# ScalarE's copies spread by an account of its work, one more transform with eight residues, and the last inverse rows moved by six products

## The chip, the cores and the metric

The kernel runs on one core of one Trainium2 chip. The metric is device time in microseconds of one launch. The core's engines run side by side, each with an instruction stream of its own: TensorE (PE, with its weight loads as PEld), VectorE (DVE), ScalarE (ACT), GpSimd (POOL) and SyncE (SP). SP, ACT and POOL also issue the DMAs.

## The reference, cut to what matters

The kernel computes the forward and the backward pass of a block with two branches: a long convolution over the sequence (branch A) and a bilinear gated unit (branch B).

```python
xn = layernorm(q)                                   # 2048 x 1024
k_shift = sum over t of k_pad[t:t+S] * shift_k[:, 3-t]
kv = k_shift * v
y  = irfft(rfft(kv, 4096) * rfft(ssm_k, 4096))[:S] + kv * ssm_D
s  = xn * y                                         # branch A
h  = (xn @ w_gate) * (xn @ w_up)                    # 2048 x 3584
g  = silu(h @ w_down)                               # branch B
out = q + s * g
# the outputs: out, and the gradients of all inputs for a given grad_out
```

## The kernel before

**Stages.** The program is a sequence of dense matmul stages on TensorE. The convolution's Fourier transforms and products, most of which are VectorE's work, run beside them. The stage around the change is the first one: the gate and up projections (`gu_unit`, 14 slabs of 256 columns of F, 16 blocks of 128 rows each), with the forward convolution (`conv_forward`) beside it. After it comes the down projection (`bm_mm`, `late_mm`), under which the last slice of the convolution ends.

**A product.** `gu_unit` takes one to four row blocks of one slab. For each it makes a *product*: eight matmuls of 128x512 into one of two PSUM buffers `psg` (L671), which ScalarE copies into `gut` (L673). TensorE can start a product only when the copy of the product two before is done. Four products on, VectorE multiplies gate by up into `hN` (recorded at L212 as `hN<-gut`), `Hd` and `GUd` are stored, and for a pair of units `turn_pair` (L694 to L706) turns `hN` on TensorE through the one PSUM tile `tr`; two ScalarE copies bring it to `hT`, which SP stores in `HTd`. The turn is put off by five products (`defer`, `flush(5)`).

**The convolution.** It goes over eight slices of 128 columns (`ds` 0 to 7). A slice needs the transform of kv (kind 0) and that of the filter row h (kind 1). Each transform has two halves: TensorE multiplies by Fourier tables into `psF` tiles (`cmm`, L234), two ScalarE copies bring a half to one of two `SP` buffers (L256 or L295), and VectorE sums them (`W<-SP`) and forms the spectrum in `KX` or `HX`. With four residues (`fwd4_half`) a transform is 32 matmuls of 128x256 and little VectorE work; with eight (`fwd8_half`) it is 16 and more VectorE work. `EIGHT` lists the transforms that use eight. After the product of both spectra (`product`) comes the inverse on VectorE (`inv_dft` or `inv8`), and then `tail`: inverse rows on TensorE into `psI` (L455) and ScalarE's copies to `yf` (L825).

**The filter row.** Before its transform, h is ordered by four ScalarE copies `hx<-U` (`h_order`, L785), turned on TensorE through `tr`, and copied back by two `hx<-tr` (`h_turn`, L809). For slice 0, `h_turn` transposes straight from the row (L800, copies L802). Both are called from the stages of `product`: `h_order` in its first four, `h_turn` in the fifth.

**What sets the order.** The convolution is a generator that yields its estimated VectorE time. `tick`, called once per product, pumps it by a fraction of the total `F_TOTAL`. That order is the program order. A scheduler may move instructions on their engines by its own estimate, except those given to `tc.keep_in_program_order`: once `PIN[0]` is set, VectorE's of the convolution, and the first matmul of each group of a transform. ScalarE's copies are not pinned.

**The end of the convolution.** When the projections end, VectorE still works on slice 7. TensorE goes on with products of the down projection: `late_mm(n)` is the n-th, two matmuls of 128x512. The inverse rows of slice 7 are issued by `step()` behind products 68 and 75 (`at`), each followed by copies to `yf` and `y_first` on ScalarE. The gates, VectorE's next stage, need these rows.

Of the kernel before, what the change touches and what calls it, by code (L numbers as in the profile page):

```python
# [10 lines left out]
ACT = mybir.ActivationFunctionType  # L11
# [8 lines left out]
def build_kernel(  # L20
# [11 lines left out]
    nc = tc.nc  # L32
# [27 lines left out]
    def ld(out, in_):  # L60
        return nc.sync.dma_start(out=out, in_=in_)
# [9 lines left out]
    def sta(out, in_):  # L71
        return nc.scalar.dma_start(out=out, in_=in_)
# [113 lines left out]
    def turn_tables(psp):  # L186

        for j in range(2):
            ps = psp.tile([P, 8, 2, P], BF16, name="psT", tag="psF")
            for r in range(8):  # L190
                for k in range(2):
                    nc.tensor.transpose(ps[:, r, k, :], T4[j][:, r, k, :], ident[:])
            nc.scalar.copy(out=TI[:, j], in_=ps[:])
            yield


# [32 lines left out]
    def cmm(ps, T, x, rs, first=None, held=False):  # L229

        xr = x.rearrange("p (c r) d -> p r c d", c=2)
        for k in range(2):
# [5 lines left out]
            if first is not None and k == 0:  # L238
                nc.tensor.matmul(ps[:, 0, 0:P], T[:, 0, 0, :], first, start=False, stop=True)

    pe_us = [0.0]

    def net(w):
# [4 lines left out]
    def fwd4_half(x, i, wp, psp, first=None):  # L248

        pe_us[0] += 1.75  # L250
        SP = wp.tile([P, 2, 2, 512], F32, name="SP", bufs=2)
        for par in range(2):
            ps = psp.tile([P, 2, 2, 256], F32, name="psF")
            cmm(ps[:, 0], T4[par], x, (i, i + 4), first if i == 0 else None, True)
            cmm(ps[:, 1], T4[par], x, (i + 2, i + 6))
            nc.scalar.copy(out=SP[:, :, par], in_=ps[:].rearrange("p s k x -> p s (k x)"))  # L256
        return SP

    def fwd4_buf(wp):
# [27 lines left out]
    def fwd8_half(x, i, SP, psp, first=None, held=False):  # L287

        pe_us[0] += 0.87
        for j in range(2):  # L290
            r = 2 * i + j
            ps = psp.tile([P, 2, 2, 256], F32, name="psF")
            cmm(ps[:, 0], T4[0], x, (r,), first if r == 0 else None, held)
            cmm(ps[:, 1], T4[0], x, (r + 4,))
            nc.scalar.copy(out=SP[:, :, j], in_=ps[:].rearrange("p s k x -> p s (k x)"))  # L295

    def fwd8(SPs, X, W, C, ahead, late=False):

# [269 lines left out]
    def halves(x):  # L568
        return x.rearrange("p b (h u) -> p h b u", h=2)
# [64 lines left out]
    later = []  # L634
    gu_mm = [None]

    def tr_tile():
        return ps_tr.tile([P, 2, 8, P], BF16, name="tr")

    def defer(fn):  # L640
# [14 lines left out]
    def gu_unit(sl, b0, n, w, tick):  # L655
# [11 lines left out]
        for i in range(n):  # L667
            q, qi = divmod(b0 + i, 4)
            ps = ps_gu.tile([P, 512], F32, name="psg")
            for dc in range(DC):  # L670
                gu_mm[0] = nc.tensor.matmul(ps[:], XNT[q][:, dc, qi * P:(qi + 1) * P],  # L671
                                            w[:, dc].rearrange("p a f -> p (a f)"), start=(dc == 0), stop=(dc == DC - 1))
            nc.scalar.copy(out=gut[:, :, i], in_=ps[:].rearrange("p (a f) -> p a f", a=2))  # L673
            flush(5)
            if i == 0:
                turn_late()
            hn[0]()
            hn[0] = nop
            tick()
        sta(GUd[sl, b0 // 8][:, :, b0 % 8:b0 % 8 + n], gut[:, :, 0:n])  # L680

        def multiply():
# [24 lines left out]

        def store(hT):
            half, rest = divmod(b0, 8)
# [30 lines left out]
    def conv_forward():  # L740
# [12 lines left out]
        def load_h(ds):  # L753
            hrow = U[5][:, 0:2048].rearrange("p (c u r) -> p c u r", c=2, r=8)
            cld(U[5][:, 0:2048], A_ssm_k[ds * P:(ds + 1) * P, :])
            S_["h", ds] = hrow
# [18 lines left out]
            yield 2.3  # L775

        def h_order(ds, part):
            if ds == 8:
                return
            hrow = S_["h", ds]  # L780
            if part == 0:
                S_["hx"] = cf.tile([P, NB, P], BF16, name="hx")
            if ds > 0:
                c, q = divmod(part, 2)
                nc.scalar.activation(S_["hx"][:, 4 * part:4 * part + 4, :], hrow[:, c, :, 4 * q:4 * q + 4].rearrange("p u r -> p r u"),  # L785
                                     ACT.Copy, scale=WSC)
                if part == 3 and ds + 1 < 8:
                    load_h(ds + 1)

        def h_turn(ds):  # L790
            if ds == 8:
                return
            hx = S_["hx"]
            pe_us[0] += 0.67
            if ds == 0:
                hrow = S_["h", 0]
                ps = tr_tile()
                for b in range(NB):
                    with tc.issue_after(tr_ln[0].ins) if b == 0 else nullcontext():
                        nc.tensor.transpose(ps[:, b // 8, b % 8, :], hrow[:, b // 8, :, b % 8], ident[:])  # L800
                    if b % 8 == 7:
                        nc.scalar.activation(hx[:, b - 7:b + 1, :], ps[:, b // 8], ACT.Copy, scale=WSC)  # L802
                load_h(1)
            else:
                ps = tr_tile()[:].rearrange("p h b x -> p h (b x)").rearrange("p h (b u) -> p h b u", u=64)
                for b in range(NB):
                    turn_halves(lambda hh: ps[:, hh, b], hx[:, b, :])
                for c in range(2):
                    nc.scalar.copy(out=halves(hx[:, 8 * c:8 * c + 8, :]), in_=ps[:, :, 8 * c:8 * c + 8])  # L809
            h_out.append(ds)  # L810

        def kvs(ds):
            return S_["kvt", ds // 2][:, :, ds % 2 * P:(ds % 2 + 1) * P]
# [1 line left out]
        def tail(ds):  # L815
            G = S_.pop(("G", ds))
            if ds < 7:
                yf = cs.tile([P, NB, P], BF16, name="yf")[:]
            else:
                yf = krow[:].rearrange("p a b d -> p (a b d)")[:, 0:NB * P].rearrange("p (b d) -> p b d", b=NB)  # L820
            for rq in range(2):
                ps = (ps_tr if cv_gone else ps_cv).tile([P, 4, 256], F32, name="psI", tag="tr" if cv_gone else "psF")
                inv_quad(G, ps, rq, ds in INV8)
                pe_us[0] += 0.9 if ds in INV8 else 1.8
                nc.scalar.copy(out=yf.rearrange("p (c r) d -> p r c d", c=2)[:, 4 * rq:4 * rq + 4], in_=rowps(ps))  # L825
# [50 lines left out]
        yield from shift(0)  # L876
        PIN[0] = True
        yield 3.9
        h_order(0, 0)
        h_turn(0)  # L880
        yield 0.1
        tl = turn_tables(ps_cv)
        sp = [half(0, S_["hx"], i, Dz[:, 0:P]) for i in range(2)]
        for ds in range(8):
# [11 lines left out]
            if ds == 0:  # L896
                yield from transform(0, 1, sp, HX, own_room(KX), lambda i: sph.append(half(0, kvs(0), i)), nop)
            else:
                yield from transform(ds, 0, sp, KX, own_room(HX), lambda i: sph.append(half(ds, S_["hx"], i, D0)), nop)
                S_["kst"] = st(KFd[ds], KX[:])  # L900
            calls = []

# [13 lines left out]
                S_["filters"] = False  # L916
            st(HFd[ds], HX[:])
            for n, w in enumerate(product(KX, HX, KX, cs, False, 0)):
                if n < 4:
                    h_order(ds + 1, n)  # L920
                else:
# [80 lines left out]
    def tick(by=1):  # L1002
        cnt[0] += by
        if cnt[0] == -4:
            pump((SHIFT_W + 4.05) / F_TOTAL)
        if cnt[0] >= -2:
            pump((SHIFT_W + (F_TOTAL - SHIFT_W) * (cnt[0] + 6.5) / (NT + 3.5)) / F_TOTAL)
# [38 lines left out]
                ld(HT0[1][:, 8:12], ht_rows(0, 24, 28))  # L1046
    assert len(h_out) == 8 and not soon
    hn[0]()

    def bm_mm(ps, ht, i, fc):  # L1050
        for dh in range(2):
# [16 lines left out]
    pss = [ps_bm.tile([P, D], F32, name="psbm") for i in range(2)]  # L1068
    with tc.issue_after(bm_first(range(4)).ins):
        flush()  # L1070
    for p_ in (ps_gu, fg, fw):
        p_.release()
    ub = pool("ub", 1, side="right")
# [752 lines left out]
```

## Time and profile before

| what | value |
|---|---|
| median of three runs | 1915.73 us (1915.4 to 1916.0) |
| the profiled execution's time | 1915.55 us |
| its span, first to last instruction | 1913.8 us |
| granted TensorE clock | 1.00 |
| products (`psg`) end | about 505 us |
| VectorE's forward convolution ends | 551.6 us |
| inverse rows of slice 7 | 561.45 and 565.34 us |

A line of the page's fifth part, or of a list of groups, gives the source line, engine, operation, tiles (written <- read), shapes and count, then the busy time and the mean of one, then the engine's idle time before them and what ended it. The costliest ScalarE groups of 100 to 505 us read so:

```profile
L673 ACT CAST gut<-psg 128x512 bf16<-128x512 f32 x131 | 76.8, 591 | 89.9 <-PE psg L671 84.7 <-remote 3.4 <-DVE m L212 1.1
L705 ACT COPY hT<-tr 128x1024 bf16<-128x1024 bf16 x46 | 44.4, 1018 | 0.5 <-PE tr L565 0.5
L256 ACT COPY SP<-psF 128x1024 f32<-128x1024 f32 x44 | 42.5, 1018 | 9.3 <-PE psF L234 6.8 <-DVE W L212 1.8 <-DVE KX L212 0.7
L785 ACT ACTIVATE hx<-U 128x512 bf16<-128x512 bf16 x28 | 31.2, 1167 | 2.5 <-DVE KX L283 2.5
```

A gut copy takes 0.59 us, every other copy about one; a product on TensorE takes 1.73 us (eight matmuls, one each 0.216). In lists in order of time a line gives start and length in us, engine, line, operation, tiles, shapes and count, and in brackets the idle time before it with what ended it.

### The profile page before, as it was taken

What the parts mean: (1) busy time and instruction counts of PE and PEld (TensorE: products, weight loads), DVE (VectorE), ACT (ScalarE), POOL (GpSimd) and SP (SyncE); (2) the same over time, 40 slices, a digit from 0 to 9 for tenths busy, and PEclk for the clock granted to TensorE, in tenths of its full rate; (3) what the DMA queues carried; (4) which work ended last, traced back from release to release, by engine and by line L of the source; (5) the groups of instructions that cost most, each with busy time, mean ns of one, the idle gap of its engine ahead of it and who ended that gap; (6) DMA issues with size and microseconds to landing.
All of it is one profiled execution on the core that took longest, in us unless ns stands there. A gap on an engine that the chain in (4) does not pass through costs nothing.

```text
span 1913.8 us, 28261 instructions
## 1 busy us (share of the span) xinstructions
PE 1890.4 (99%) x11350; PEld 1007.9 (53%) x11491; DVE 1550.6 (81%) x1711; ACT 664.0 (35%) x955; POOL 332.8 (17%) x465
## 2 busy tenths in 40 slices
PE   8999999999999999999999999999999999999999
PEld 5555555545544456666666665664444444444444
DVE  8999999999978556887999999999995205788862
ACT  5765666656433233432222222222222102110121
POOL 5121211201103220001031221111212101111120
PEclk9999999999999999999999999999999999999999
DMA  8777766769769997677887698585887999989862
GB/s 292 273 240 235 259 219 219 234 224 298 249 207 301 326 321 231 209 238 230 273 266 262 223 265 265 182 286 177 226 246 171 228 201 196 186 183 190 187 181 89
DMA packets 425107, 444.35 MB, mean 232 GB/s; under 512 B 268400, under 2 KB 342796, under 8 KB 410512
## 3 DMA queue, kind: packets, MB, share of 16 engines
q1 hardware_dynamic: 367504, 239.03, 46.4%
q0 software_dynamic: 41152, 174.15, 28.9%
q10 hardware_dynamic: 16320, 29.36, 4.1%
q8 instruction: 90, 1.47, 0.3%
q14 instruction: 41, 0.34, 0.1%
HBM read 193.87 MB, written 189.84 MB: 200 GB/s over the span
## 4 chain that ended last, share of the span: by engine, by line
PE 94%; DVE 2%; ACT 2%; issue 1%; DMA 0%; SPq 0%; ACTq 0%
PE psb L1517 20%; PE psx L1662 20%; PE psg L671 17%; PE psb L1500 10%; PE psbm L1052 10%; PE psb L1600 9%; PE psF L234 3%; PE tr L565 1%; PE psI L455 1%; DVE W L212 1%; ACT hx L785 1%; PE psY L1211 1%; PE psY L445 1%; PE psx L1600 1%; DVE bst L578 0%
## 5 line engine op out<-in xcount | busy, mean ns | idle before, releaser
L671 PE MATMUL psg<-wslab,U 128*128 128x512 bf16 x1727 | 398.0, 380 | 12.2 <-ACT gut L673 3.8
L1517 PE MATMUL psb<-U,U 128*128 128x512 bf16 x1792 | 397.1, 379 | 0.0
L1662 PE MATMUL psx<-U,dgut 128*128 128x512 bf16 x1505 | 331.0, 379 | 1.6
L1662 PEld LDWEIGHTS <-dgut 128*128 128x128 bf16 x1792 | 174.9, 98 | 211.8
L1517 PEld LDWEIGHTS <-U 128*128 128x128 bf16 x1792 | 174.9, 98 | 198.3
L671 PEld LDWEIGHTS <-U 128*128 128x128 bf16 x1792 | 172.0, 98 | 203.8 <-issue 9.8
L1500 PE MATMUL psb<-wdt,U 128*128 128x256 bf16 x1792 | 205.6, 273 | 0.0
L1500 PEld LDWEIGHTS <-U 128*128 128x128 bf16 x1792 | 174.8, 98 | 29.6
L212 DVE TENSOR_TENSOR W<-W 128x1024 f32<-128x1024 f32 (+1 forms) x189 | 186.5, 1003 | 4.0
L1600 PE MATMUL psb<-U,U 128*128 128x512 bf16 x797 | 176.1, 380 | 0.9
L1522 ACT CAST wb<-psb 128x512 bf16<-128x512 f32 x112 | 65.7, 587 | 315.3 <-PE psb L1517 307.5
L1267 DVE SCALAR_TENSOR_TENSOR dkp<-dkT,kT 128x1024 bf16<-128x1024 bf16 (+2 forms) x64 | 78.3, 1224 | 94.5 <-DMA dkT<-DKSHd 92.8
L1052 PE MATMUL psbm<-U,ht 128*128 128x512 bf16 x658 | 145.1, 379 | 0.7
L1600 PEld LDWEIGHTS <-U 128*128 128x128 bf16 x896 | 87.2, 98 | 104.5
L1694 ACT ACTIVATE dx_t<-dxn 128x1024 bf16<-128x1024 f32 x15 | 15.9, 1057 | 324.9 <-DVE dxn L212 320.1
L673 ACT CAST gut<-psg 128x512 bf16<-128x512 f32 x156 | 91.4, 592 | 101.9 <-PE psg L671 96.3
L1052 PEld LDWEIGHTS <-ht 128*128 128x128 bf16 x672 | 65.5, 98 | 78.3
L212 DVE TENSOR_TENSOR U<-U,dht 128x2048 bf16<-128x2048 bf16 x56 | 68.3, 1221 | 46.7 <-ACT dht L1502 46.7
L1502 ACT CAST dht<-psb 128x512 bf16<-128x512 f32 x112 | 65.7, 588 | 116.1 <-PE psb L1500 115.0
L66 POOL DMA_DIRECT2D Hd<-hN x54 | 37.1, 687 | 256.8 <-DVE hN L212 254.0
L1641 ACT CAST wbs<-psb 128x512 bf16<-128x512 f32 x51 | 29.9, 587 | 145.4 <-PE psb L1600 134.4
L212 DVE TENSOR_TENSOR W<-SP 128x1024 f32<-128x1024 f32 x64 | 74.3, 1219 | 1.5 <-ACT SP L295 0.8
(265 smaller groups left out, 2361.0 us busy)
## 6 DMA issues: line engine op xcount, KB each, us to landing
U<-GUd SPq DMA_DIRECT2D x28, 1024.0 KB, 9.2
DGd<-U SPq DMA_DIRECT2D x28, 1024.0 KB, 5.9
GUd<-gut ACTq DMA_DIRECT2D x39, 512.0 KB, 6.5
out_dram<-wb SPq DMA_DIRECT2D x112, 128.0 KB, 4.4
U<-Hd SPq DMA_DIRECT2D x14, 1024.0 KB, 5.9
Hd<-hN POOLq DMA_DIRECT2D x54, 256.0 KB, 4.4
HTd<-hT SPq DMA_DIRECT2D x24, 512.0 KB, 4.0
ht<-HTd SPq DMA_DIRECT2D x18, 512.0 KB, 7.8
```

What stands on the lines that cost most here:

```text
L212: pinned(V.tensor_tensor(o, a, b, op))
L234: mm = nc.tensor.matmul(ps[:, k].rearrange("p (c d) -> p c d", c=2), T[:, r, k, :], xr[:, r], start=(n == 0), stop=(n == len(rs) - 1 and ( ...
L671: gu_mm[0] = nc.tensor.matmul(ps[:], XNT[q][:, dc, qi * P:(qi + 1) * P], w[:, dc].rearrange("p a f -> p (a f)"), start=(dc == 0), stop=(dc ...
L673: nc.scalar.copy(out=gut[:, :, i], in_=ps[:].rearrange("p (a f) -> p a f", a=2))
L1052: mm = nc.tensor.matmul(ps[:, dh * 512:(dh + 1) * 512], ht(fc)[:, i * P:(i + 1) * P], WD[fc // 4][:, fc % 4, dh * 512:(dh + 1) * 512], sta ...
L1267: ins = V.scalar_tensor_tensor(prod[:].rearrange("p r d -> p (r d)")[:, lo:H], dkT[:, 0, lo:H], 1.0, kT[:, 0, 13 + m + lo:13 + m + H], op0 ...
L1500: nc.tensor.matmul(ps[:, x * SLW:(x + 1) * SLW], DBMT[2 * hf + g][:, dc, (b % 4) * P:(b % 4 + 1) * P], wdt[:, dc, :], start=(dc == 0), sto ...
L1502: nc.scalar.copy(out=dht[:, 2 * e:2 * e + 2].rearrange("p b f -> p (b f)"), in_=ps[:])
L1517: nc.tensor.matmul(ps[:], XN[b // 4][:, b % 4, dc * P:(dc + 1) * P], dgus[b // 8][:, :, b % 8], start=(b == 0), stop=(b == NB - 1))
L1522: nc.scalar.copy(out=wb[:, dc % 2].rearrange("p a f -> p (a f)"), in_=ps[:])
L1600: nc.tensor.matmul(ps, h[:, f, b, :], DBM[b // 4][:, b % 4, dh * 512:(dh + 1) * 512], start=(b == 0), stop=(b == NB - 1))
L1662: nc.tensor.matmul(ps[:, dh * 512:(dh + 1) * 512], t[n][:, f, i * P:(i + 1) * P], WGU[n][:, f, dh * 512:(dh + 1) * 512], start=(n == 0 and ...
```

## The change

It has three parts.

1. **An account of ScalarE's work.** `act_us` grows with each slow copy (`copied`) and falls by 2.0 per product, to which 0.6 for the gut copy is added (`one_tick`). The copies of h (`h_order`, `h_back`) and of `hT` no longer stand where their data is made: they go into a list `slow`, and after each product `run_slow` issues from it while the account stays under 2.2. The turn of h, too, is issued from that list. Copies of `hT` go to its front. A copy out of the tile `tr` that is still held is issued at once when `tr` is wanted again (`tr_tile`), and one of h when its transform wants it (`hx`). With `PIN[0]` set, these copies and those of gut, SP, TI and yf are kept in program order.
2. **`EIGHT`** gains `(5, 0)`: kv of slice 5 is transformed with eight residues.
3. **`at`** becomes `(74, 81)`: the two groups of inverse rows of slice 7 stand six products of the down projection later.

```diff
+    act_us = [0.0]
+    slow = []
+
+    def copied(us, ins=None):
+        act_us[0] += us
+        if ins is not None and PIN[0]:
+            tc.keep_in_program_order(ins)
+
+    def one_tick():
+        act_us[0] = max(0.0, act_us[0] - 2.0) + 0.6
+
+    def run_slow(all_=False):
+
+        while slow and (all_ or act_us[0] + slow[0][0] < 2.2):
+            us, fn = slow.pop(0)
+            copied(us)
+            fn()
...
-            nc.scalar.copy(out=SP[:, :, par], in_=ps[:].rearrange("p s k x -> p s (k x)"))
+            copied(1.0, nc.scalar.copy(out=SP[:, :, par], in_=ps[:].rearrange("p s k x -> p s (k x)")))
...
+    tr_held = []
+
     def tr_tile():
+        while tr_held:
+            slow.pop(0)[1]()
         return ps_tr.tile([P, 2, 8, P], BF16, name="tr")
...
-            nc.scalar.copy(out=gut[:, :, i], in_=ps[:].rearrange("p (a f) -> p a f", a=2))
+            one_tick()
+            copied(0.0, nc.scalar.copy(out=gut[:, :, i], in_=ps[:].rearrange("p (a f) -> p a f", a=2)))
             flush(5)
...
             tick()
+            run_slow()
...
-            for g in range(2):
-                nc.scalar.copy(out=halves(hT[:, 2 * g:2 * g + 2].rearrange("p q a i s -> p (q a i) s")), in_=ps[:, :, 8 * g:8 * g + 8])
-            ht_st[0] = ld(to.rearrange("q f a s -> f q (a s)"), hT[:].rearrange("f q a i s -> f q (a i s)"))
+
+            def copy(g):
+                copied(0.0, nc.scalar.copy(out=halves(hT[:, 2 * g:2 * g + 2].rearrange("p q a i s -> p (q a i) s")),
+                                           in_=ps[:, :, 8 * g:8 * g + 8]))
+                if g == 1:
+                    tr_held.clear()
+                    ht_st[0] = ld(to.rearrange("q f a s -> f q (a s)"), hT[:].rearrange("f q a i s -> f q (a i s)"))
+            tr_held.append(True)
+            slow.insert(0, (1.0, lambda: copy(1)))
+            slow.insert(0, (1.0, lambda: copy(0)))
...
-    EIGHT = ((0, 0), (0, 1), (6, 0), (7, 0), (7, 1))
+    EIGHT = ((0, 0), (0, 1), (5, 0), (6, 0), (7, 0), (7, 1))
...
+        def h_rows(ds):
+            if ds < 8:
+                pe_us[0] += 0.67
+                for part in range(4):
+                    slow.append((1.15, lambda part=part: h_order(ds, part)))
+                slow.append((0.0, lambda: h_turn(ds)))
+                for c in range(2):
+                    slow.append((1.0, lambda c=c: h_back(ds, c)))
...
+        def hx(ds):
+            while len(h_out) <= ds:
+                slow.pop(0)[1]()
+            return S_["hx"]
...
             for n, w in enumerate(product(KX, HX, KX, cs, False, 0)):
-                if n < 4:
-                    h_order(ds + 1, n)
-                else:
-                    h_turn(ds + 1)
+                if n == 1:
+                    h_rows(ds + 1)
                 yield w
...
-    at = (68, 75)
+    at = (74, 81)
```

The first row of h (slice 0) has a function of its own, `h_first`, with the work of the old `h_turn(0)`. What is left of `slow` is issued at the end of the projections (`run_slow(True)`).

More of the change, by code (lines that the diff above doesn't have):

```diff
@@ L192, in turn_tables @@
                     nc.tensor.transpose(ps[:, r, k, :], T4[j][:, r, k, :], ident[:])
-            nc.scalar.copy(out=TI[:, j], in_=ps[:])
+            copied(1.9, nc.scalar.copy(out=TI[:, j], in_=ps[:]))
             yield
@@ L294, in fwd8_half @@
             cmm(ps[:, 1], T4[0], x, (r + 4,))
-            nc.scalar.copy(out=SP[:, :, j], in_=ps[:].rearrange("p s k x -> p s (k x)"))
+            copied(1.0, nc.scalar.copy(out=SP[:, :, j], in_=ps[:].rearrange("p s k x -> p s (k x)")))
     def fwd8(SPs, X, W, C, ahead, late=False):
@@ L777, in h_order @@
         def h_order(ds, part):
-            if ds == 8:
-                return
-            hrow = S_["h", ds]
             if part == 0:
                 S_["hx"] = cf.tile([P, NB, P], BF16, name="hx")
[L783 to L788, printed above, removed]
@@ L790, in h_turn @@
-        def h_turn(ds):
[L791 to L803, printed above, removed]
-            else:
-                ps = tr_tile()[:].rearrange("p h b x -> p h (b x)").rearrange("p h (b u) -> p h b u", u=64)
-                for b in range(NB):
-                    turn_halves(lambda hh: ps[:, hh, b], hx[:, b, :])
-                for c in range(2):
-                    nc.scalar.copy(out=halves(hx[:, 8 * c:8 * c + 8, :]), in_=ps[:, :, 8 * c:8 * c + 8])
-            h_out.append(ds)
+            c, q = divmod(part, 2)
@@ new lines, in h_order @@
+            copied(0.0, nc.scalar.activation(S_["hx"][:, 4 * part:4 * part + 4, :],
+                                             S_["h", ds][:, c, :, 4 * q:4 * q + 4].rearrange("p u r -> p r u"), ACT.Copy, scale=WSC))
+            if part == 3 and ds + 1 < 8:
+                load_h(ds + 1)
+        def h_turn(ds):
+            ps = tr_tile()[:].rearrange("p h b x -> p h (b x)").rearrange("p h (b u) -> p h b u", u=64)
+            for b in range(NB):
+                turn_halves(lambda hh: ps[:, hh, b], S_["hx"][:, b, :])
+            S_["hps"] = ps
+            tr_held.append(True)
@@ new lines, in h_back @@
+        def h_back(ds, c):
+            copied(0.0, nc.scalar.copy(out=halves(S_["hx"][:, 8 * c:8 * c + 8, :]), in_=S_["hps"][:, :, 8 * c:8 * c + 8]))
+            if c == 1:
+                tr_held.clear()
+                h_out.append(ds)
+        def h_rows(ds):
[4 more added lines that the diff above has]
+                slow.append((0.0, lambda: h_turn(ds)))
+                for c in range(2):
+                    slow.append((1.0, lambda c=c: h_back(ds, c)))
@@ new lines, in h_first @@
+        def h_first():
+            hx = S_["hx"] = cf.tile([P, NB, P], BF16, name="hx")
+            hrow = S_["h", 0]
+            ps = tr_tile()
+            for b in range(NB):
+                with tc.issue_after(tr_ln[0].ins) if b == 0 else nullcontext():
+                    nc.tensor.transpose(ps[:, b // 8, b % 8, :], hrow[:, b // 8, :, b % 8], ident[:])
+                if b % 8 == 7:
+                    nc.scalar.activation(hx[:, b - 7:b + 1, :], ps[:, b // 8], ACT.Copy, scale=WSC)
+            load_h(1)
+            h_out.append(0)
@@ L824, in tail @@
                 pe_us[0] += 0.9 if ds in INV8 else 1.8
-                nc.scalar.copy(out=yf.rearrange("p (c r) d -> p r c d", c=2)[:, 4 * rq:4 * rq + 4], in_=rowps(ps))
+                copied(1.05, nc.scalar.copy(out=yf.rearrange("p (c r) d -> p r c d", c=2)[:, 4 * rq:4 * rq + 4], in_=rowps(ps)))
                 if ds == 7 and rq == 0:
@@ L878, in conv_forward @@
         yield 3.9
-        h_order(0, 0)
-        h_turn(0)
+        h_first()
         yield 0.1
@@ L898, in conv_forward @@
             else:
-                yield from transform(ds, 0, sp, KX, own_room(HX), lambda i: sph.append(half(ds, S_["hx"], i, D0)), nop)
+                yield from transform(ds, 0, sp, KX, own_room(HX), lambda i: sph.append(half(ds, hx(ds), i, D0)), nop)
                 S_["kst"] = st(KFd[ds], KX[:])
@@ L918, in conv_forward @@
             for n, w in enumerate(product(KX, HX, KX, cs, False, 0)):
-                if n < 4:
-                    h_order(ds + 1, n)
-                else:
-                    h_turn(ds + 1)
+                if n == 1:
+                    h_rows(ds + 1)
                 yield w
@@ L1048, in build_kernel @@
     hn[0]()
+    run_slow(True)
     def bm_mm(ps, ht, i, fc):
@@ L1070, in build_kernel @@
         flush()
+        run_slow(True)
     for p_ in (ps_gu, fg, fw):
```

## The prediction

> **What bounds the kernel now.** I read the page's busy line, then busy time by stage, then the waits that ended TensorE's idle time in the stage that the change touches, then stretches in order of time.
>
> ```profile
> PE 1890.4 (99%) x11350; PEld 1007.9 (53%) x11491; DVE 1550.6 (81%) x1711; ACT 664.0 (35%) x955; POOL 332.8 (17%) x465
> ...
> PEclk9999999999999999999999999999999999999999
> ```
> ```profile
> 125.00:555.00 430.00, 424.02 (x3039) 223.64 (x3092) 423.84 (x395) 251.60 (x333) 62.87 (x89) 1.00 0.73 244
> ```
> TensorE sets the time, at full clock. But from 125 to 555 us (columns: PE, PEld, DVE, ACT, POOL) VectorE is as full: 423.84 of 430. ScalarE, 59% busy, can only hurt by its order. The waits (us, times, longest) from 50 to 570 us:
> ```profile
> PE psg L671 <- ACT gut L673: 2.9, 4, 1.5
> PE psg L671 <- ACT U L673: 2.5, 3, 1.4
> ```
> Seven waits, 5.4 us: a product (eight matmuls) finds both psg buffers uncopied. One of them, TensorE first, then ScalarE:
> ```profile
> 109.17 1.89 PE L671 MATMUL psg<-wslab,U 128*128 128x512 bf16 x8 [1.39 <-ACT U L673]
> ```
> ```profile
> 105.75 1.14 ACT L785 ACTIVATE hx<-U 128x512 bf16<-128x512 bf16 x1
> 106.79 1.85 ACT L193 COPY TI<-psT 128x2048 bf16<-128x2048 bf16 x1
> 108.53 0.59 ACT L673 CAST U<-psg 128x512 bf16<-128x512 f32 x1
> ```
> Three microseconds of slow copies stood ahead of the copy that TensorE needed. The others (0.45 and 0.67 beside it, 0.38, 1.50, 0.81, and 0.20 at 75 us) have the same cause.
>
> **The change, part by part.**
> *Fewer matmuls.* kv of slice 5 takes 16 matmuls of 128x256 in place of 32. Eight such (psI) start at 508.43 and the next product at 509.30: 0.109 each. 16 x 0.109 = **-1.74**. The number of SP copies stays.
>
> *Waits removed.* In the changed order of ScalarE's stream the groups of hxo, hT and yf copies that stood ahead of one gut copy now stand singly. All seven waits lose their cause: **-5.4**. If the spreading failed: 0.
>
> *Waits added at the start.* Pinned in program order, the second hx copy of slice 0 now stands ahead of product 24's copy (counted from 0), and four SP copies ahead of product 25's. Before:
> ```profile
> 66.32 0.61 ACT L673 CAST gut<-psg 128x512 bf16<-128x512 f32 x1
> 67.79 0.59 ACT L673 CAST gut<-psg 128x512 bf16<-128x512 f32 x1 [0.86 <-PE psg L671]
> 68.28 1.03 ACT L802 ACTIVATE hx<-tr 128x1024 bf16<-128x1024 bf16 x1
> 70.06 3.76 ACT L295 COPY SP<-psF 128x1024 f32<-128x1024 f32 x4 [0.76 <-PE psF L234]
> ```
> Product 24's copy now starts at 69.3, not 66.3. Product 26 cannot run six matmuls (1.3) between 68.1 and 69.5 as before, and product 27 waits for product 25's copy, 73.8 to 74.4, some 0.7. Following both on to the end of product 28, which is 77.0 before, I get 77.8 with eight psF matmuls (0.87) still to do: 1.7 later, 1.9 with the 0.2 counted as removed. **+1.9**; bounds 0 (the copies overlap what TensorE waits for anyway) and 3.8 (the whole SP row).
>
> *Waits added where transposes force held copies.* At products 94 and 150 the order is hx, hx, hT, gut: a turn of h, held in PSUM, is emptied just before the next turn of hN. Copies of 0.59 + 2 x 1.02 keep that turn until 2.7 us after a product's end, its 32 transposes take 0.65, hT 1.0, gut 0.6: 5.0, when TensorE, after two products and the transposes (2 x 1.73 + 0.65 = 4.1), wants the buffer. 0.8 each, **+1.6**; bounds 0 and 2 x 1.4 (the longer waits of before).
>
> *VectorE.* Eight residues cost it more: kv of slice 7 takes from 494.19 to 505.98 after its SP sums, less 0.6 for an hN between: 11.1; slice 5 with four residues 365.44 to 369.98: 4.5. **+6.6 of VectorE**. It can win back only its own idle time. The larger pieces:
> ```profile
> 118.41 0.69 DVE L212 TENSOR_TENSOR hN<-gut 128x1024 bf16<-128x1024 bf16 x1 [1.09 <-ACT gut L673]
> ...
> 127.74 0.69 DVE L212 TENSOR_TENSOR hN<-gut 128x1024 bf16<-128x1024 bf16 x1 [1.65 <-ACT gut L673]
> ```
> with 0.48 at 246.6 and 0.17 at 312.7: 3.4. So its forward work ends at 551.60 + 6.6 - 3.4 = 554.8, and its clock reaches TensorE where an SP buffer (two) must be read before the next half is copied. The last such place is h of slice 7 (ScalarE, VectorE, TensorE):
> ```profile
> 494.55 1.93 ACT L295 COPY SP<-psF 128x1024 f32<-128x1024 f32 x2
> ```
> ```profile
> 489.04 4.63 DVE L212 TENSOR_TENSOR W<-SP 128x1024 f32<-128x1024 f32 x4
> ```
> ```profile
> 494.79 1.89 PE L671 MATMUL psg<-wslab,U 128*128 128x512 bf16 x7
> 496.51 1.04 PE L234 MATMUL psF<-hx,TF 128*128 128x256 bf16 x8
> ```
> The first buffer is free at 489.04 + 2.35 = 491.39, 3.2 before the copy. After: 491.39 + 6.6 + 0.6 (one hN now stands ahead of it) - 3.4 = 495.2. TensorE would come there with -1.74 - 5.4 + 1.9 + 1.6 = -3.6, and one product later in its order (+1.73): 494.55 + 1.73 - 3.6 = 492.7. The copies wait 2.5. Of that 0.5 is free (the second copy ended at 496.48, the matmuls that need its PSUM began half way into the row at 496.51). **+2.0**. Queued behind the waiting copy are gut copies, for which psg waits. Bounds: 0 (VectorE wins back 2 us more) and 5.4 (none won back). At the same place in slices 3 to 6 the same count gives waits of 0 to 1.0, within 0.35 of free.
>
> *Last inverse rows.* No work added: twelve matmuls (2.6 us) change places with them.
> ```profile
> 549.10 2.50 DVE L283 SCALAR_TENSOR_TENSOR HX<-W 128x512 bf16<-128x512 f32 x4
> ```
> ```profile
> 561.45 1.04 PE L455 MATMUL psI<-HX,TI 128*128 128x256 bf16 x8
> ```
> Slack 9.9 us before. After: rows at 561.45 + 2.6 - 1.6 = 562.4, inverse done at 554.8: 7.6 left, cost 0. The first gate on VectorE (566.47) comes 1.0 later; VectorE is 58% busy from 600 to 700, which hides it. Without that cover the price is that 1.0.
>
> *Moved DMAs.* Loads of h rows go later on POOL's queue, past Hd stores and k and v loads; they have most of a slice (50 us). HTd stores go one or two products later on SP's queue, past a slab load's half at places; a slab has 16 products (28 us) to land. Cost 0; a late slab would show as TensorE waiting for a DMA, of which 50 to 570 us has none.
>
> **Sum:** -1.7 - 5.4 + 1.9 + 1.6 + 2.0 = -1.6. The profiled execution took 1915.55 (its span 1913.8 plus 1.75 around it; the median of the runs is 1915.73). Behind 566 us TensorE idles little until its tail, so the gain passes through: 1915.55 - 1.6 = **1913.9**.
>
> **Rivals.**
> 1. *VectorE does not hold it back, and the start costs less.* For: at that place 3.2 us of slack stood, and the two added bunches may fall beside other waits. Against: VectorE's 423.84 of 430. Without the 2.0: 1911.9; without the start's 1.9 too: 1910.0; with no added wait at all (-7.1): 1908.4.
> 2. *Slower: ScalarE and VectorE hold each other.* With everything pinned, two SP copies that wait for VectorE keep a gut copy behind them, and if VectorE's next instruction is the hN of that gut, it idles for 2 x 1.01 + 0.59 = 2.6, and all after it is later by that. Places: the h halves of slices 3 to 7, five. For: in slices 3 to 5 the SP copies began only 0.1 to 0.9 after their buffer was free, and in slices 3 and 4 they now come two products (3.5 us) earlier. Against: VectorE reaches hN some 2 to 5 us after its gut copy. It decides from the first full case (2.6 against 1.6): three make 1921.7, five 1926.9. [...]
> 3. *It doesn't do what it says:* the account only moves the bunches, and the added waits equal the removed ones and the matmuls. 1915.5, within 0.8.
>
> **How the numbers follow.** Forecast (-0.8 to -3.4) 0.41; rival 1 (-3.4 to -7.1) 0.34; rival 2 0.15; rival 3 0.10. A measurement of this kernel can tell about 0.2%, 3.8 us, from no change. Faster by more: most of rival 1, 0.30; slower by more: rival 2 from two and a half cases on, 0.12; the rest 0.58. The range 1909.8 to 1918.0 leaves out a tenth on each side: rival 1's far end and rival 2 from two cases on. The forecast's own range is 1912.1 to 1914.8.
>
> **What would show it.** The waits of psg for gut from 100 to 450 us fall from 5.2 to under 2.5; about 2 us of new wait near 66 to 77 us; 0.8 each near products 94 and 150; VectorE idle under 1 us from 125 to 550 and its last inverse instruction near 555; SP copies of h of slice 7 waiting for VectorE and TensorE for them, about 2; rows near 562 with no wait. Wrong if VectorE waits for gut copies (rival 2), or if SP copies of h do not wait at all (rival 1).

## The result, and the profile after

The changed kernel is slower: 1926.22 us, the median of five runs (1920.61 to 1927.32), against 1915.40 before (five runs, 1915.08 to 1916.0). The ratio is 1.0048, with a 95% interval of 1.0033 to 1.0064: a small loss, under 2%, but clear of the noise. The profiled execution is the quickest of the five, 1920.61 us with a span of 1918.8. What it shows has to account for 5.1 us (1920.61 less the 1915.55 of the profiled execution before), and something else must make the other runs 2 to 7 us longer than it.

The page's busy line of the changed kernel, then its busy time by stage (columns: PE, PEld, DVE, ACT, POOL, clock):

```profile
PE 1899.6 (99%) x11475; PEld 1008.7 (53%) x11475; DVE 1556.1 (81%) x1723; ACT 667.1 (35%) x955; POOL 332.9 (17%) x465
```
```profile
125.00:555.00 430.00, 422.28 (x3046) 219.74 (x3045) 425.34 (x401) 253.98 (x332) 62.58 (x89) 1.00 0.72 241
```

VectorE is busy for 425.3 of 430 us, 1.5 more than before. The waits that ended TensorE's idle time, 50 to 575 us (us, times, longest):

```profile
PE tr L583 <- ACT hx L812: 3.6, 5, 0.7
PE tr L583 <- DVE hN L212: 3.4, 1, 3.4
PE psF L234 <- ACT hx L847: 1.1, 1, 1.1
PE psg L693 <- ACT gut L696: 0.6, 1, 0.6
PE psg L693 <- ACT U L696: 0.6, 1, 0.6
```

The seven waits of `psg` are gone. Four kinds stand in their place. The start (1.1 of `psF`, 0.65 of `psg`) and the wait of 0.6 at product 150 were predicted. The turns of h were not, and neither was one wait of 3.4 us of the last turn of hN for VectorE. The end of the projections in order of time, changed kernel:

```profile
504.86 0.37 SPq L61 DMA_DIRECT2D U<-in_B_w_down_dram  x1
...
505.35 1.02 ACT L730 COPY hT<-tr 128x1024 bf16<-128x1024 bf16 x1
505.48 0.52 ACTq L72 DMA_DIRECT2D GUd<-gut  x1
506.39 0.37 SPq L61 DMA_DIRECT2D HTd<-hT  x1
```
```profile
511.29 0.69 DVE L212 TENSOR_TENSOR hN<-gut 128x1024 bf16<-128x1024 bf16 x1
...
512.03 0.61 PE L583 MATMUL tr<-ident,hN 64*128 64x64 bf16 x16 [3.41 <-DVE hN L212]
...
514.53 1.93 ACT L730 COPY hT<-tr 128x1024 bf16<-128x1024 bf16 x2 [8.16 <-DMA HTd<-hT]
...
517.64 1.04 PE L473 MATMUL psI<-HX,TI 128*128 128x256 bf16 x8
```

The same place in the kernel before:

```profile
503.57 0.36 SPq L61 DMA_DIRECT2D HTd<-hT  x1
505.17 0.37 SPq L61 DMA_DIRECT2D U<-in_B_w_down_dram  x1
...
508.25 0.69 DVE L212 TENSOR_TENSOR hN<-gut 128x1024 bf16<-128x1024 bf16 x1
508.43 1.04 PE L455 MATMUL psI<-HX,TI 128*128 128x256 bf16 x8
...
510.56 0.64 PE L565 MATMUL tr<-ident,hN 64*128 64x64 bf16 x32
```

Two things are late. VectorE's last hN begins 3.0 us later (511.29 for 508.25), and its turn, which before came 2.3 us behind the start of that hN with eight psI matmuls ahead of it in TensorE's order, now stands ahead of them and blocks TensorE. (e7 below, which has the eight residues and no account, shows the same new order: psI at 515.37, behind the turn at 511.40.) And the store of hT is issued 2.8 us later (506.39 for 503.57), now behind the load of a down-projection slab and a store of `gut`. From issue to landing (last column) it takes twice as long; changed kernel, then before:

```profile
HTd<-hT SPq DMA_DIRECT2D x1, 512.0 KB, 8.0
```
```profile
HTd<-hT SPq DMA_DIRECT2D x1, 512.0 KB, 4.0
```

hT has one buffer, so the next copy to it, the one at 514.53, starts only after that landing. ScalarE idles 8.16 us before it, of which 1.9 lie behind the turn that it copies (512.03 + 0.61); in this execution TensorE does not wait for it. The wait at 512.03 has a second price. The granted clock behind it (the first of the last three columns):

```profile
512.00:515.00 3.00, 2.97 (x22) 1.32 (x23) 3.00 (x3) 0.47 (x1) 0.67 (x1) 0.50 1.08 431
515.00:518.00 3.00, 3.00 (x16) 1.44 (x15) 2.97 (x5) 1.46 (x2) 0.00 (x0) 0.93 0.54 208
```

The half clock lasts from 512.01 to 515.42, 3.41 us, in which the weight loads of 128x512 matmuls come 0.43 us apart (512.98, 513.40, 513.83), where one such matmul takes 0.216 at full clock, and so costs half of that, 1.7. Up to product 222 TensorE stands 0.3 us ahead of before; 3.4 + 1.7 later it is 4.8 behind, and its inverse rows come at 568.82 and 572.71, where 561.45 + 2.6 and 565.34 + 2.6 would be level. That is the loss of the profiled execution.

### The profile page after: what moved, and what is told of

Same layout as the page of the kernel before. It is cut to its first block, busy times and chain, and to the rows that moved or that the text cites. A ratio compares the mean times of both kernels' runs of the same rounds, so it can differ in the third digit from the quotient of the medians.

```text
span 1918.8 us, 28375 instructions
## 1 busy us (share of the span) xinstructions
PE 1899.6 (99%) x11475; PEld 1008.7 (53%) x11475; DVE 1556.1 (81%) x1723; ACT 667.1 (35%) x955; POOL 332.9 (17%) x465
## 4 chain that ended last, share of the span: by engine, by line
PE 82%; DVE 13%; issue 3%; DMA 2%; ACT 1%; SPq 0%; DVEq 0%; ACTq 0%
PE psx L1705 20%; PE psb L1560 20%; PE psb L1543 10%; PE psg L693 10%; PE psb L1643 9%; PE psbm L1094 6%; DVE W L212 4%; PE psF L234 2%; DVE HX L212 2%; DVE KX L212 1%; DVE U L212 1%; DVE m L212 1%; DVE hN L212 1%; PE psY L1254 1%; PE psY L463 1%
## 5 line engine op out<-in xcount | busy, mean ns | idle before, releaser
L693 PE MATMUL psg<-wslab,U 128*128 128x512 bf16 x1792 | 403.9, 379 | 4.1 <-DMA wslab<-in_B_w_gate_dram 1.6
L1737 ACT ACTIVATE dx_t<-dxn 128x1024 bf16<-128x1024 f32 x15 | 15.9, 1057 | 325.4 <-DVE dxn L212 325.4
```

## The experiments

Each kernel ran beside the kernel before, whose median lay between 1915.14 and 1915.76. (In two expectations "195 us" is a slip and stands for nothing.)

| run | edit | median (us) | ratio to before, 95% |
|---|---|---|---|
| e1 | the changed kernel again | 1924.56 | 1.0050 [1.0038, 1.0062] |
| e2 | four residues for slice 5 | 1935.03 | 1.0100 [1.0087, 1.0113] |
| e3 | last turn of hN later | 1917.23 | 1.0007 [0.9998, 1.0016] |
| e4 | that wait filled | 1926.59 | 1.0057 [1.0045, 1.0069] |
| e5 | hT's store on ScalarE's queue | 1934.84 | 1.0100 [1.0086, 1.0114] |
| e6 | e5 with four residues | 1938.88 | 1.0121 [1.0106, 1.0137] |
| e7 | before, with eight residues alone | 1920.04 | 1.0023 [1.0014, 1.0032] |
| e8 | four mends | 1916.28 | 1.0006 [0.9997, 1.0015] |
| e9 | hT's copies not held | 1920.93 | 1.0030 [1.0018, 1.0041] |
| e10 | e9 with four residues | 1919.16 | 1.0020 [1.0011, 1.0028] |
| e11 | e8, hT's copies not held | 1914.12 | 0.9994 [0.9985, 1.0003] |
| e12 | e11 with four residues | 1910.92 | 0.9979 [0.9970, 0.9988] |
| e13 | e10, turn of h moved | 1913.32 | 0.9990 [0.9982, 0.9999] |
| e14 | e10, start unpinned | 1917.88 | 1.0014 [1.0005, 1.0023] |
| e15 | e12, inverse rows back | 1910.77 | 0.9977 [0.9967, 0.9986] |

### e1 and e2: the change again, and without the eight residues

e1 has no edit. e2:

```diff
-    EIGHT = ((0, 0), (0, 1), (5, 0), (6, 0), (7, 0), (7, 1))
+    EIGHT = ((0, 0), (0, 1), (6, 0), (7, 0), (7, 1))
```

> The changed kernel once more, as measure for the others and for its spread (1920.6 to 1927.3 in five runs). Theory A (the last turn of hN on TensorE, behind the first 16 matmuls of the down projection, waits for VectorE's last hN, and the idle time halves the clock afterwards): the profile shows one wait of 3 to 4 us before that turn and a granted clock of 0.5 for some microseconds behind it; a slower run shows a longer half-clock stretch or a second one, all else the same. Theory B (ScalarE's pinned order costs the time in the projections): a slower run shows more or longer waits between 60 and 500 us.

> The change without its second part: kv of slice 5 with four residues again (16 more matmuls, 1.74 us; 6.6 us less VectorE). Theory A: the last hN is ready some 3 us or more earlier and the turn stands behind eight psI and five more matmuls as in the kernel before, so no wait there and no half clock: near 1917 (before 1915.4, -5.4 of waits removed, +1.9 at the start, +3.6 of turns of h that wait for their last copy, about +0.6 elsewhere: 1916.1) and as narrow in spread as before. Theory B: it stays near the changed kernel, 1920 to 1927.

e1 took 1922.72 to 1931.24. In its profile (1923.64) the turn waits 2.6 us for hN and then psI 1.2 us more for hT: the copy of hT waits 9.9 us for the store of hT in place of 8.2. So the landing differs between these two executions of one kernel.

e2 was expected to be faster than the changed kernel, and was 10 us slower. The end wait is gone, as it should be with less work for VectorE, but in mid-stage the copies of hT wait for their store. In order of time, e2:

```profile
342.09 0.37 SPq L61 DMA_DIRECT2D HTd<-hT  x1
...
351.03 1.01 ACT L730 COPY hT<-tr 128x1024 bf16<-128x1024 bf16 x1 [8.16 <-DMA HTd<-hT]
351.94 0.59 ACT L696 CAST gut<-psg 128x512 bf16<-128x512 f32 x1
...
352.58 6.23 PE L693 MATMUL psg<-wslab,U 128*128 128x512 bf16 x16 [6.20 <-ACT gut L696]
```

ScalarE's stream is pinned, so the gut copy stands behind the waiting hT copy, and TensorE idles 6.20 us here and 3.79 at 161 us, each with 6.8 us of half clock that begin 1.5 and 1.2 us before the wait ends. In the changed kernel the order in mid-stage is another: its store of 156.45 is followed by the next hT copy at 170.35, where in e2 the store of 153.07 is followed by one at 159.61. The theory that VectorE's extra work alone was to blame fell here: a second cause is in the account itself.

### e3 and e4: the last turn of hN

e3 issues the last turn behind 32 of the matmuls that follow it, not 16; e4 leaves it in place and puts 16 matmuls on an idle tile ahead of it (e4 does work that nothing uses).

```diff
-    with tc.issue_after(bm_first(range(4)).ins):
+    with tc.issue_after(bm_first(range(8)).ins):
...
-    fc_ = 4
+    fc_ = 8
```

> The changed kernel with the last turn of hN put behind 32 matmuls of the down projection in place of 16 (nothing left out). Theory A: TensorE works while VectorE ends hN; wait of 3.4 and half clock (1.7) both go: 1920.6 - 5.1 = 1915.5, spread under 1 us. Theory B: unchanged, 1920 to 1927.

> The changed kernel with 16 matmuls of 128x512 (3.45 us) before the last turn of hN whose result nobody reads, so that TensorE is not idle there. Within theory A this parts the wait from the clock: the wait's time is still spent, the half clock is not. If the clock costs 1.7 us and the spread: near 1919, spread under 1 us. If the wait alone costs it: as the changed kernel, 1920.6 or more. Theory B: 3.4 us above the changed kernel, 1924 or more.

e3 took 1917.23, some 7 us less than e1: the wait and the half clock are gone. It stays 1.7 above its theory, and its runs lie 4.6 us apart, not 1. e4 took as long as the unedited kernel. Its lines:

```profile
512.66 0.64 PE L583 MATMUL tr<-ident,hN 64*128 64x64 bf16 x32
...
517.51 1.93 ACT L730 COPY hT<-tr 128x1024 bf16<-128x1024 bf16 x2 [10.15 <-DMA HTd<-hT]
...
519.48 1.03 PE L473 MATMUL psI<-HX,TI 128*128 128x256 bf16 x8 [4.13 <-ACT hT L730]
```

The turn waits for nothing, and the whole loss comes back at 519 us, where psI needs the PSUM tile that hT's copy has not emptied. So two late things stand behind each other, and the second is the store of hT. e3 does without both because its psI goes ahead of the turn.

### e5 and e6: is it the queue?

```diff
-                    ht_st[0] = ld(to.rearrange("q f a s -> f q (a s)"), hT[:].rearrange("f q a i s -> f q (a i s)"))
+                    ht_st[0] = sta(to.rearrange("q f a s -> f q (a s)"), hT[:].rearrange("f q a i s -> f q (a i s)"))
```

`sta` issues on ScalarE's queue. e6 has four residues as well.

> The changed kernel, with the store of hT (to HTd) issued on ScalarE's queue in place of SP's; nothing else. Theory S (the store stands behind a slab load on SP's queue, hT has one buffer, so the next copies to hT wait for the landing): the stores land about 3 to 4 us after issue in place of 2 to 12, no hT copy waits for a DMA, no psI wait for hT at 519 us; the wait of 3.4 us of the last turn of hN for VectorE with its half clock stays, so the median falls only to 1919 to 1921, and the runs lie closer together (within 3 us, where those of the changed kernel spread over 7 to 8). Rival (the spread of landings comes from the load on the DMA engines, not from the order on the queue): landings stay at up to 8 to 12 us, median 1923 to 1927.

> As the run before, and kv of slice 5 transformed with four residues again, so that what stays of the change is the account, the hT store on ScalarE's queue and the last inverse rows. Theory S: the psg waits of 3.8 and 6.2 us that the changed kernel with four residues had behind hT copies (195 us and 1935 in all) are gone, and with VectorE earlier there is no end wait either: 1915.55 - 5.4 (psg waits) + 1.8 (start) + 3.6 (turns of h) + 0.6 (product 150) = 1916, 1915 to 1918. Rival (those waits were VectorE's or ScalarE's own lateness): they stay, 1925 or more.

Theory S fell. On the other queue the same store lands 10.5 us after its issue (e5):

```profile
HTd<-hT ACTq DMA_DIRECT2D x1, 512.0 KB, 10.5
```
```profile
527.32 1.93 ACT L730 COPY hT<-tr 128x1024 bf16<-128x1024 bf16 x2 [10.59 <-DMA HTd<-hT]
...
529.30 1.86 PE L473 MATMUL psI<-HX,TI 128*128 128x256 bf16 x8 [5.45 <-ACT hT L730]
```

Both kernels are slower than the changed one. e5 also loses 2.95 us at 484.71, behind a gut copy that waited 5.64 us for a store of `gut`, which goes by the same queue. In e5 and in the changed kernel a 1 MB load (SP's queue) and a 512 KB store of `gut` (ScalarE's) are issued 1.5 and 0.9 us ahead of that store, the last but one of hT. Where neither is issued just ahead of it, it lands sooner: in 4.0 us before, and in 4.2 in e10, where from 506.5 to 507.8 us only a store of hN goes out beside it. So what is in flight when the store is issued explains the landings better than SP's queue does; but e5 does not rule the queue out, since there the store stands behind the store of `gut` on its own. What was measured is no gain: 10.5 us on ScalarE's queue against 8.0 on SP's.

### e7: the eight residues alone

The kernel before, with (5, 0) added to `EIGHT`.

> The kernel before with the eight residues for kv of slice 5 and nothing else. Theory V (VectorE's last hN comes later by what eight residues add, 6.6 us less its idle time): the last hN lies 2 to 4 us later than 508.25, the last turn of hN waits for it 1 to 3 us less what the order at the end covers, and the matmuls save 1.7: 1914 to 1919, depending on whether the wait is long enough for the clock to fall; the stores of hT stay ahead of the slab loads, so no hT copy waits for a DMA. Rival (the lateness comes from the account of ScalarE's work, not from VectorE): no wait at the last turn, 1914.

It is 4.9 us slower than before, 1920.04, above the expected 1914 to 1919. The largest price is again at the last turn (e7):

```profile
511.40 0.41 PE L565 MATMUL tr<-ident,hN 64*128 64x64 bf16 x16 [3.26 <-DVE hN L212]
```

The last hN begins at 510.65, 2.4 us later than before, the turn waits 3.26 and the clock is at half from 512 to 515. No hT copy waits for a DMA here: without the account the store keeps its place. Another 1.37 us go at 309.52, where `psF` waits for an SP copy that itself waited 2.84 us for VectorE. That is how the prediction thought VectorE would reach TensorE, at another slice than it named.

### e8: four mends

hT's store on ScalarE's queue as in e5; the last turn as in e3; and

```diff
         while slow and (all_ or act_us[0] + slow[0][0] < 2.2):
+            if slow[0][0] == 0.0 and n and not all_:
+                break
+            n += 1
...
-        if ins is not None and PIN[0]:
+        if ins is not None and PIN[0] and APIN[0]:
```

The first keeps the turn of h from being issued in the same product as the copy that it reads (`n` starts at 0 in each call); the second pins ScalarE's copies only once `APIN[0]` is set, at the end of slice 0's transforms.

> The changed kernel with four mends: hT's store on ScalarE's queue; the last turn of hN behind 32 in place of 16 of the matmuls after it; the turn of h issued at the earliest one product after the copy that it reads; ScalarE's copies pinned in program order only after the start of slice 0, so that the start has the order of the kernel before. Theory: 1915.55 - 1.7 - 5.4 + 0.6 (product 150) + 0 to 1 (the rest of the turns of h and small waits) = 1909 to 1911, faster than the kernel before by 0.2 to 0.35%. Rival (VectorE sets the end, so that what TensorE gains is lost at the last turn again): a wait of over 1.5 us for hN or psI near 510 to 520 us, 1914 or more.

1916.28, not the 1909 to 1911 of the theory, with runs within 1.2 us of each other. TensorE was 2.1 us ahead at product 204 and 0.4 at 213. Between them a copy of `gut` waits for a store of `gut` to land, and `psg` waits for that copy (e8):

```profile
475.11 0.58 ACT L702 CAST gut<-psg 128x512 bf16<-128x512 f32 x1 [3.62 <-DMA GUd<-gut]
...
475.74 1.89 PE L699 MATMUL psg<-wslab,U 128*128 128x512 bf16 x8 [1.24 <-ACT gut L702]
```

The next product waits 0.44 more. So hT is not the only tile whose late store holds up ScalarE.

### e9 to e12: not holding hT's copies

```diff
-            tr_held.append(True)
-            slow.insert(0, (1.0, lambda: copy(1)))
-            slow.insert(0, (1.0, lambda: copy(0)))
+            copied(2.0)
+            copy(0)
+            copy(1)
```

e9 is the changed kernel with this alone, e10 has four residues too. e11 is e8 with this and the store back on SP's queue, e12 is e11 with four residues.

> The changed kernel, with the two copies of hT issued right behind their turn as before (counted in the account, but not held). Theory H (what makes the stores of hT late is that their copies are held: the store comes one or two products later and falls into the burst of loads and stores at a product's end, and the next copies of hT, which need the one buffer back, come sooner after it): no hT copy waits for a DMA, no wait of psI for hT, the runs lie within 4 us; the wait of some 3 us of the last turn of hN and its half clock stay, so 1918 to 1921, as with eight residues alone. Rival (the transfers are late whatever the order, the DMA engines being 73% busy): hT copies still wait for HTd in some slices, 1923 or more.

> As the run before, and four residues for kv of slice 5, so that of the change stay the account for hx, yf, TI and SP, and the last inverse rows. Theory H: the waits of 3.8 and 6.2 us of the changed kernel with four residues (195 us of busy time apart, at 161 and 353 us) are gone, no wait for hN at the end, since VectorE has less to do: 1915.55 - 5.4 + 1.8 (start) + up to 3.6 (turns of h, where they still follow the copy they read) + up to 2 (hT behind hx at five places) = 1912 to 1918. Rival: those waits stay or move, 1922 or more.

> The kernel of four mends, but with hT's copies not held and their store back on SP's queue. Theory F (from about 475 us VectorE's work is the floor, so with eight residues nothing that TensorE gains ahead of it counts): as the four mends, 1915 to 1917, TensorE ahead by 2 to 3 us until product 207 and by under 1 at product 213. Rival (its loss at 475 us came from the late hT): 1911 to 1914.

> As the run before, with four residues for kv of slice 5: VectorE has some 4 to 6 us less to do, 16 matmuls (1.74 us) are added again. Theory F: the floor is off, TensorE keeps at product 222 what it gained, 1 to 4 us ahead of before: 1911.5 to 1914.5. Rival (the floor is not VectorE): behind the kernel before it by the 1.74, 1916 to 1919.

Theory H held in its main point: with eight residues 3.6 us less than e1 (1920.93 for 1924.56; 3.1 by their distances to the kernel before, 5.7 and 8.8), with four 15.9 less than e2 (1919.16 for 1935.03, though above the expected 1912 to 1918), and in none of e9 to e12 does an hT copy wait for a DMA. Holding those copies was a mistake in the account. They free PSUM for TensorE, and their store frees the one hT buffer. Each product of delay brings the store nearer to the next copy, and at the end it puts the store behind a load. The first half of the theory, that the hold makes the landings late, is shown at the end alone (8.0 us for 4.0): from 100 to 555 us the median time to landing is 4.0 us with the hold and without it, in the changed kernel and before, though single stores took up to 11.6 us with it and up to 8.5 without. What the hold takes away is distance. From the issue of a store to the next copy it left as little as 4.2 us in the changed kernel; before, it is never under 7.6 from 100 us on.

e11 against e12 shows what VectorE's extra work costs. TensorE's waits in e11 (all but the two shortest kinds), then all in e12, 50 to 575 us:

```profile
PE psF L234 <- ACT SP L280: 2.3, 3, 0.9
PE psF L234 <- DVE kv L212: 1.0, 1, 1.0
PE tr L759 <- ACT hT L761: 0.6, 1, 0.6
PE tr L589 <- DVE hN L212: 0.5, 1, 0.5
PE psg L699 <- ACT gut L702: 0.4, 1, 0.4
```
```profile
PE tr L759 <- ACT hT L761: 0.6, 1, 0.6
PE tr L589 <- ACT hT L736: 0.4, 2, 0.2
```

With eight residues the waits lead to VectorE (SP copies wait 3.9 us for it in e11, 1.2 in e12). With four there are 16 matmuls more (1.74 us) and the kernel is 3.2 us faster, a little better than expected, and 0.21% faster than the kernel before. e8 is 2.2 us longer than e11, from which it differs in the hold of hT and in the queue of its store. Theory F as it was put, with VectorE as the floor from 475 us on, fell: e11 keeps 2.9 us at product 213 where e8 kept 0.4, so what e8 lost there, 1.7 us, are the waits of 1.24 and 0.44 behind the store of `gut`.

### e13 to e15: the terms apart

e13 is e10 with the edit of `run_slow` shown under e8, e14 is e10 with the edit of `APIN`, and e15 is e12 with

```diff
-    at = (74, 81)
+    at = (68, 75)
```

> As the changed kernel with hT not held and four residues (1919.16), with the turn of h issued at the earliest one product behind the copy that it reads; nothing else. The trace had each of seven turns of h last 2.07 us in place of 0.64, with two matmuls of 0.22 of a product inside: 1.0 lost each. Theory: 7 x 1.0 = 7 us less, 1912 to 1913. Rival (only the idle time that the list of waits names is lost, 4.3 us): 1914.5 to 1915.5.

> As the changed kernel with hT not held and four residues (1919.16), with ScalarE's copies pinned only from the end of slice 0's transforms on; nothing else. Theory: the start's two waits (1.11 and 0.65) go, 1917.0 to 1917.7. Rival (the slack at VectorE takes it up): 1918.5 or more.

> The best kernel so far (1910.92) with the last inverse rows back at their old place in TensorE's order, at products 68 and 75 of that list in place of 74 and 81; nothing else. Theory (the rows wait for nothing in either place): 1910.4 to 1911.4, no wait at the rows. Rival (the later place was needed): TensorE waits for HX at the rows, 1912 or more.

The turns of h cost 5.8 us (1919.16 to 1913.32), more than the 4.3 that the list of waits names in e10 and less than the 7 estimated. One of them in the changed kernel:

```profile
161.72 0.52 PE L583 MATMUL tr<-ident,hx 64*128 64x64 bf16 x24
162.18 0.61 PE L693 MATMUL psg<-wslab,U 128*128 128x512 bf16 x2
162.31 1.14 ACT L812 ACTIVATE hx<-U 128x512 bf16<-128x512 bf16 x1
163.51 0.29 PE L583 MATMUL tr<-ident,hx 64*128 64x64 bf16 x8 [0.72 <-ACT hx L812]
```

The turn is in `slow` with cost 0, right behind the last ordering copy, and issued in the same call. Its last eight transposes read what that copy (162.31 to 163.45) is still writing. Before, all 32 took 0.64 us in one piece. All seven turns of h are split like this, in the changed kernel and in e10.

The start costs 1.3 (1919.16 to 1917.88, a little less than expected), and the rows' place nothing that shows (1910.77 and 1910.92).

## Why the prediction was wrong, by its own steps

The forecast of 1913.9 (1909.8 to 1918.0) was wrong in sign. Step by step:

- **Waits removed, -5.4: right.** The seven are gone, and those listed instead have other causes.
- **Start, +1.9: right**, 1.11 + 0.65 = 1.76 in the trace and 1.3 between e10 and e14. The two added waits of 0.8 came to one of 0.62, at product 150.
- **Fewer matmuls, -1.74:** the traces of e11 and e12 count 11475 and 11491 matmuls, 16 apart; no run shows the time alone.
- **VectorE +6.6, and 3.4 won back: right.** Its last hN came 3.0 later, and its forward work ended at 554.62, predicted 554.8.
- **The step that failed: who waits for VectorE.** "The last such place is h of slice 7" followed VectorE's clock to the SP buffers alone. TensorE also reads hN. Its last turn had 1.6 us from the end of hN to its start (508.94 to 510.56) and stands, in the changed order, ahead of the psI that covered it. Cost: 3.41 and 1.7 of half clock in the profiled run; e7, which has the eight residues alone, is 4.9 slower. The wait of the SP copies, +2.0, did not come, since TensorE was not ahead there; where it is (e7, e11), such waits come, in earlier slices.
- **The second that failed: "Moved DMAs … Cost 0".** It asked only what the stores of hT do to the slab loads behind them. It did not ask who waits for the stores: the next hT copies, through the one buffer, and all that is pinned behind these. Before, the smallest time between a landing and the next copy was 3.6 us from 100 us on; after, it was 0.1. The hold is worth 3.6 us with eight residues (e1 to e9). Whether it also makes the spread is not shown: the runs of e1 lie 8.5 us apart and those of e9 3.6, but so do those of e4 (3.5), where the copies are held.
- **A cost that was not in the sum at all: the turns of h**, 5.8 by e13. The prediction read where the account puts ScalarE's copies, and not what TensorE reads right behind the last of them.
- **Last inverse rows, 0: right** (e15).

With the missing terms the sum is -1.74 - 5.4 + 1.8 + 0.6 + 5.8 + 5.1 = +6.2, against 5.1 in the profiled run. The excess arises before the end: without the 5.1 these terms put TensorE 1.1 us behind at product 222, and it stood 0.3 ahead. The other runs of the changed kernel are 2 to 7 us longer. Late stores are one reason: in e1's profile psI waits 1.2 us for one, and e9 is 3.6 below e1. What makes up the rest is not shown.

None of the rivals was it. The slower one had the right engines (ScalarE in order, VectorE full) but the wrong place: VectorE's only listed wait from 125 to 555 us is one of 0.3, for an SP copy. That its five cases give 1926.9, next to the measured 1926.2, is luck.

The account as such is worth having: with its copies of hx, yf, TI and SP spread, hT not held, the turn of h one product later, the last turn of hN later and the start unpinned, the kernel takes 1910.8 to 1910.9, 4.3 to 4.4 us (0.2%) less than before, and without the eight residues. The gain is made in the projections: e12 is 4.9 us ahead of the kernel before at product 222, ahead of the last turn.

## What to carry to other kernels

When an instruction is held back, list who waits for its result and for the buffer that it frees, on every engine and through DMAs: a store that goes two products later is the next copy's wait if the tile has one buffer (8.16 us of ScalarE here). When an engine that is off the path gets work, follow its lateness to every reader on the engine that sets the time, above all where the order around the last reader has changed too. And place a consumer by when its producer ends, not by when it is issued: a cost of 0 in an account says "at once".

## What the runs showed of the hardware

An idle time of TensorE can cost more than its length, since in some of these runs the granted clock fell to half with it: in the changed kernel it is 1.00 from 510 to 512 us and 0.50 from 512.01 to 515.42, 3.41 us. In the other runs below, the granted clock of the stretches around the wait gives as long a half clock, or twice that:

| wait of TensorE, from 50 us on (us) | half clock with it (us) |
|---|---|
| 1.24 (e8), 1.37 (e5, e7), 1.50 (before) | none |
| 1.82 (e9), 2.59 (e1), 2.95 (e5), 3.26 (e7), 3.41 (changed kernel), 4.13 (e4) | 3.4 |
| 3.79 and 6.20 (e2) | 6.8 |

In e6, whose longest wait is 8.9 us, the mean clock of the whole execution was 0.996, as in e2; in the changed kernel it was 0.999. In e5, with waits of 2.95 and 5.45 us, the clock of 480 to 530 us was 0.93.

The length alone does not decide it: 3.79 brought 6.8, and 4.13 brought 3.4. Nor does the half clock begin where the wait ends: in e2 1.2 and 1.5 us before, in e1 1.05 after. What sets its start and its length is not shown, nor how long TensorE must idle for it: 1.50 us (before) brought none, 1.82 (e9) brought 3.4.

The time from issue to landing of one 512 KB store (hT's) ranged from 2.9 to 11.6 us within one stage of the changed kernel, with the DMA engines busy 72% on average from 125 to 555 us.
